# Converting weight pieces in pairs of 1024 columns, with the integer sums on GpSimd: a fused attention and feed-forward kernel on one Trainium2 core

## The chip, the cores and the metric

The kernel runs on 1 core of one Trainium2 chip. A core has TensorE (PE: matrix products; PEld is its loading of weights), VectorE (DVE), ScalarE (ACT), GpSimd (POOL) and SyncE (SP, which here issues nearly all DMAs). Each engine works through its own list of instructions in order and waits on semaphores for the others. SBUF is the on-chip memory of 128 partitions, PSUM the accumulators that TensorE writes. The metric is device time in microseconds (us); a run's time is compared as a median of several.

## The reference: what is computed

Eight batches of eight heads of linear attention without softmax, normalized per head, and then a feed-forward block with a squared relu on 4608 tokens (d_model 512, d_ff 2048):

```python
kv = np.einsum('bhsd,bhse->bhde', k, v)
out = np.einsum('bhsd,bhde->bhse', q, kv)
rms = np.sqrt(np.mean(out * out, axis=-1, keepdims=True) + 1e-06)
x = (out / rms * g_norm)            # then (B,H,S,D) -> (B*S, H*D)
h = x @ w_in
g = np.maximum(h, 0.0) ** 2
y = g @ w_out
```

q, k, v are float32 of shape (8, 8, 576, 64). The two weight matrices, 512 x 2048 and 2048 x 512, come as float64. [...] 

## The kernel before

**Stages.** The tokens are worked through in nine strips of 512. While strip 0 goes through the first product (`up_first`, L892 to L907), the weights are loaded and converted; from strip 1 on the products use Strassen-like sums of blocks of the weights, which are computed once, on the way, and stored in DRAM for streaming (`w_out`, `w_deep`). From about 132 us on, one strip follows another in the same way until the end.

**Pieces.** The weights are cut into 32 pieces of 128 partitions x 512 numbers (`sources`, L233): 16 of w_in (four column groups g, four row chunks) and 16 of w_out (two halves eh, eight j). A piece of raw 64-bit words takes 4 KB per partition; the pool `raw` has eight places, so SP loads up to eight pieces ahead (`load_piece`, L237; `load_more`, L286). The first four pieces are converted one at a time among the work of strip 0's attention (`first_piece`, L600). The other 28 are converted two at a time by `convert_pieces` (L277), 14 pairs, which I number 2 to 15 as the pieces go.

**The conversion of a piece.** ScalarE makes the absolute value of the high word, read as a float, into a tile `w_c` (L254), and the scaled low word, rounded to an integer, in place of the raw low word (L258). VectorE then does four operations (L266 to L275): clamp, shift and mask, take in the sign bits of the high word, and add the integer from the low word. The last is the integer sum; its result is the float32 number, put where it is needed. On VectorE this sum shows in the profile as an operation on 1024 halves of words (CUSTOM_DVE_ANT_0 on uint16). In `convert_pieces` the four operations of the two pieces alternate: first of one, first of the other, second of one, and so on. ScalarE is sent its work one pair ahead of VectorE.

**What the pieces are for.** Pairs 2 to 7 are w_in: pair 2 and 3 are group 1, pairs 4 and 5 group 2, pairs 6 and 7 group 3. A unit of `up_first` (16 units, each of four products with 512 columns) reads one group, the first two products the group's first pair, the other two its second. A unit's PSUM tile comes from a pool of four (`fpsum`), so a unit can't begin before the relu and the two squares of the unit four earlier (L905, L907, on ScalarE) have emptied theirs. Pairs 8 to 11 are the first half of w_out (`pieces_out`), stored into free parts of the `w_in` tile and used as weights directly. Pairs 12 to 15 are the second half (`sums_out`, L312): each piece is converted into a tile `wt`, and four differences of 128 x 256 per piece (L317 to L323; the profile shows them at L292, the helper `minus`) give the blocks that strips use; four of them go to DRAM by four DMAs a pair (L325).

**Order.** The order of instructions on every engine is written out by hand. In strip 0's loop (L1376 on) step i runs unit i, and the conversion of a pair is put behind the units 0 to 3, ahead of the units 4 to 9, and behind the units 11 and 13 to 15 (L1380, L1408, L1468). After unit 15 come the products with w_out (`down`, L997), and with them on VectorE the sums of activations (L886), norms of the next tokens, further sums of weights (`w_t`, `w_in`), and the additions of results (L1031).

Of the kernel before, what the change touches and what calls it, by code (L numbers as in the profile page):

```python
# [10 lines left out]
FP32 = mybir.dt.float32  # L11
I32 = mybir.dt.int32
U32 = mybir.dt.uint32
I64 = mybir.dt.int64
AF = mybir.ActivationFunctionType
ALU = mybir.AluOpType
# [4 lines left out]
def kernel(  # L21
# [34 lines left out]
    nc = tc.nc  # L56
    P = 128
# [4 lines left out]
    NP = H // 2  # L62
# [27 lines left out]
    c_pool = ctx.enter_context(tc.tile_pool(name="c", bufs=6))  # L90
    conv = ExitStack()
    xt_pool = conv.enter_context(tc.tile_pool(name="xt", bufs=1))
    raw_pool = conv.enter_context(tc.tile_pool(name="raw", bufs=8))
    spare_pool = conv.enter_context(tc.tile_pool(name="spare", bufs=1))
    wtmp = conv.enter_context(tc.tile_pool(name="wtmp", bufs=4))
    psums = ExitStack()
    fpsum = psums.enter_context(tc.tile_pool(name="fpsum", bufs=4, space=bass.MemoryType.PSUM))
    opening = ExitStack()
# [110 lines left out]
    def drip_queries():  # L209
# [5 lines left out]
    KH, FH, DH = NP // 2, d_ff // 2, d_model // 2  # L215
    FQ = FC // 2
    WN = 512
    NG = FQ // 2

    w_in = wpool.tile([P, KH, NG, 7, WN // 2], FP32, name="w_in")  # L220

    w_out = dram.tile([7, P, 2, FQ, P], FP32, name="w_out")
# [5 lines left out]
    w_out_11, w_out_21, w_out_t1 = w_first = [  # L228
        w_in[:, :, :, b].rearrange("p k g e -> p (k g) e") for b in (4, 5, 6)
    ]  # L230
    w_in_v = moe_w_in.rearrange("(kc p) (b g f) -> kc g p b f", p=P, b=2, g=NG)
    w_out_v = moe_w_out.rearrange("(b j p) (eh e) -> eh j p b e", p=P, b=2, eh=2)
    sources = [w_in_v[kc, g] for g in range(NG) for kc in range(NP)]  # L233
    sources += [w_out_v[eh, j] for eh in range(2) for j in range(FQ)]
    raw = []

    def load_piece():  # L237
        if len(raw) < len(sources):
            t = raw_pool.tile([P, 2, WN // 2], I64, name="raw", tag="raw")
            nc.sync.dma_start(out=t, in_=sources[len(raw)])  # L240
            raw.append(t)


    LEAST, MOST = 2.0**-15, float.fromhex("0x1.DFFFFEp+16")

    words, acted = {}, [0]

    def convert_on_act(i, parts=(0, 1)):
        view = lambda dt: raw[i].bitcast(dt).rearrange("p b (n two) -> p b n two", two=2)
        low, high, high_f = view(U32)[:, :, :, 0], view(I32)[:, :, :, 1], view(FP32)[:, :, :, 1]  # L250
        r = view(I32)[:, :, :, 0]
        if 0 in parts:
            c = wtmp.tile([P, 2, WN // 2], FP32, name="w_c", tag="w_c")
            nc.scalar.activation(c, high_f, AF.Abs)  # L254
            words[i] = c, r, high

        if 1 in parts:
            nc.scalar.activation(r, low, AF.Copy, scale=2.0**-29)  # L258

    def conversion(i, dest, eng=nc.vector):  # L260

        c, r, high = words.pop(i)
        ci = c.bitcast(I32)


        yield eng.tensor_scalar(out=c, in0=c, scalar1=LEAST, scalar2=MOST, op0=ALU.max, op1=ALU.min)  # L266

        yield nc.vector.tensor_scalar(
            out=ci, in0=ci, scalar1=3, scalar2=0x3FFFFFFF, op0=ALU.logical_shift_left, op1=ALU.bitwise_and
        )  # L270

        yield nc.vector.scalar_tensor_tensor(
            out=ci, in0=high, scalar=-(2**30), in1=ci, op0=ALU.bitwise_and, op1=ALU.bitwise_or
        )
        yield nc.vector.tensor_tensor(out=dest.bitcast(I32), in0=ci, in1=r, op=ALU.add)  # L275

    def convert_pieces(ids, dests):  # L277

        for i in range(acted[0], min(ids[-1] + 3, len(sources))):
            convert_on_act(i)  # L280
            acted[0] = i + 1
        for _ in zip(*[conversion(i, dest) for i, dest in zip(ids, dests)]):
            pass
        load_more(ids[-1] + 1)

    def load_more(end):  # L286

        while len(raw) < min(end + 8, max(len(sources) - 4, end + 4), len(sources)):
            load_piece()

    def minus(eng, out, a, b):
        eng.tensor_tensor(out=out, in0=a, in1=b, op=ALU.subtract)  # L292

    def pieces_in(i):
        g, kc = divmod(i, NP)
        b = kc // KH * 2
        convert_pieces((i, i + 1), [w_in[:, kh, g, b : b + 2] for kh in range(KH)])

    def sums_in(g):

# [5 lines left out]
        minus(nc.vector, a21, a11, a21)  # L306

    def pieces_out(j):
        dest = lambda j: w_in[:, j // NG, j % NG, 4:6]
        convert_pieces((NG * NP + j, NG * NP + j + 1), [dest(j), dest(j + 1)])  # L310

    def sums_out(j):  # L312
        js = (j, j + 1)
        t = [raw_pool.tile([P, 4, DH], FP32, name="wt", tag="raw") for _ in js]
        convert_pieces([NG * NP + FQ + j for j in js], [x[:, 0:2, :] for x in t])
        for x, j in zip(t, js):
            minus(nc.vector, w_out_t1[:, j, :], x[:, 0], w_out_11[:, j, :])  # L317
        for x, j in zip(t, js):
            minus(nc.vector, x[:, 2], x[:, 1], w_out_t1[:, j, :])
        for x in t:  # L320
            minus(nc.vector, x[:, 0], x[:, 1], x[:, 0])
        for x, j in zip(t, js):
            minus(nc.vector, x[:, 3], w_out_21[:, j, :], x[:, 2])  # L323
            for e in range(2):
                nc.sync.dma_start(out=w_out[3:7, :, e, j].rearrange("b p e -> p b e"), in_=x[:, :, ts(e, P)])  # L325

    conversions = [(pieces_in, i) for i in range(0, NG * NP, 2)]
    conversions += [(pieces_out, j) for j in range(0, FQ, 2)] + [(sums_out, j) for j in range(0, FQ, 2)]
    converted = [NP // 2]

# [25 lines left out]
    for p in range(2, NP):  # L356
        load(0, p, nc.sync, "q")
        load_piece()
        load(0, p, nc.sync, "kv")
        next(to_load)  # L360
# [239 lines left out]
    def first_piece(i, n):  # L600

        if i not in first_steps:
            first_steps[i] = conversion(
                i, w_in[:, i % KH, 0, i // KH * 2 : i // KH * 2 + 2], nc.gpsimd if i else nc.vector
            )
        for _ in range(n):
            next(first_steps[i])
# [74 lines left out]
    def sums_x(s):  # L682
# [10 lines left out]

    act, T, K, Q, N, F, piece = (
        convert_on_act, transposed_query, key_value, first_queries, first_normalized, first_features, first_piece
    )
    U = first_up
    size, low = (lambda i: (act, (i, (0,)))), (lambda i: (act, (i, (1,))))
# [7 lines left out]
    def query_pairs(b):  # L706
        first_n = b // 2 * PAIR + (C if b % 2 else 0)
        ns = list(range(first_n, first_n + C + b % 2))
        return [ns[i : i + 2] for i in range(0, len(ns), 2)]
# [9 lines left out]
    T, K, last = transposed_query, key_value, query_pairs(1)[2]  # L719
# [624 lines left out]
    attend(ready[0])  # L1344
    opening.close()
    apsum = psums.enter_context(tc.tile_pool(name="apsum", bufs=2, space=bass.MemoryType.PSUM))
    for i in range(NP, NP + 2):
        convert_on_act(i)
    acted[0] = NP + 2
    for s in range(N_STRIP):  # L1350
        attend(ready[s])
        if s == DEEP_UP - 1:
# [23 lines left out]
        for i, (w, fn, a) in enumerate(steps):  # L1376
# [33 lines left out]
            if s:  # L1410
                clock[0] += 3.2 if i >= n_up else 2.2 if s == DEEP else 1.2
                soon = tiles_due and tiles_due[0][2][0] // NT == s + 1
                if i == n_up + 10:
                    while tiles_due and tiles_due[0][2][0] // NT == s + 1:
                        _, f, a = tiles_due.popleft()
# [38 lines left out]
            n = i + 1 - (n_up - 6)  # L1454
# [44 lines left out]
```

## Time and profile before

| what | value |
|---|---|
| three runs | 871.0, 872.51, 872.37 us; median 872.37 us |
| profiled execution | span 867.8 us from the first to the last instruction (the page gives no other time for it), 4.6 us below the median of the runs |
| granted TensorE clock | 1.00 in every stage |
| HBM read and written | 197.66 MB and 36.70 MB |
| conversions in pairs | from about 31 to 95 us of the span |

How to read it: PE is TensorE's products, PEld its weight loads, POOL is GpSimd. In a timeline row the first number is the start in us from the first instruction, the second the time from start to end, then engine, line of the kernel, operation, output<-input, shapes, and xN where N instructions of one kind follow each other; what stands in brackets is idle time ahead of it and what ended it. A row of waits tells which line of which engine waited for what: total in us, times, longest. The chain of waits follows the work back from the last instruction, at each step to what released it; its rows are start, duration, what.

### The profile page before, as it was taken

What the parts mean: (1) busy time and instruction counts of PE and PEld (TensorE: products, weight loads), DVE (VectorE), ACT (ScalarE), POOL (GpSimd) and SP (SyncE); (2) the same over time, 40 slices, a digit from 0 to 9 for tenths busy, and PEclk for the clock granted to TensorE, in tenths of its full rate; (3) what the DMA queues carried; (4) which work ended last, traced back from release to release, by engine and by line L of the source; (5) the groups of instructions that cost most, each with busy time, mean ns of one, the idle gap of its engine ahead of it and who ended that gap; (6) DMA issues with size and microseconds to landing.
All of it is one profiled execution on the core that took longest, in us unless ns stands there. A gap on an engine that the chain in (4) does not pass through costs nothing.

```text
span 867.8 us, 32590 instructions
## 1 busy us (share of the span) xinstructions
PE 858.3 (99%) x14176; PEld 803.7 (93%) x14176; DVE 721.5 (83%) x1236; ACT 352.1 (41%) x805; POOL 316.2 (36%) x321
## 2 busy tenths in 40 slices
PE   8999999999999999999999999999999999999998
PEld 7445888889999999999999999999999999999998
DVE  3999998879887996789689977897889777975887
ACT  5799251320048303750356034901491148102810
POOL 1100003630459223730574045704470447145700
PEclk9999999999999999999999999999999999999999
DMA  9998997999999997989788979997668856885583
GB/s 312 301 335 251 288 376 233 296 323 361 276 261 261 346 328 235 232 311 336 213 244 272 336 244 258 294 317 260 213 221 300 305 161 220 291 286 195 177 311 124
DMA packets 169470, 236.47 MB, mean 273 GB/s; under 512 B 78704, under 2 KB 133744, under 8 KB 161008
## 3 DMA queue, kind: packets, MB, share of 16 engines
q1 hardware_dynamic: 169024, 234.33, 83.6%
q8 instruction: 111, 1.82, 0.9%
q14 instruction: 31, 0.25, 0.1%
q10 hardware_dynamic: 304, 0.07, 0.0%
HBM read 197.66 MB, written 36.70 MB: 270 GB/s over the span
## 4 chain that ended last, share of the span: by engine, by line
PE 83%; DVE 7%; ACT 5%; DMA 4%; issue 1%; SPq 0%; DVEq 0%; ACTq 0%
PE ps_A L854 35%; PE ps_B L854 31%; PE ps_C L854 5%; PE ps_A L859 4%; PE kv_ps L437 2%; PE x_ps L473 2%; PE ps_B L859 2%; DVE w_t L292 1%; ACT raw L258 1%; ACT w_c L254 1%; DMA w_blk<-w_deep 1%; DMA w_deep<-w_t 1%; DVE wt L292 1%; DMA first_qkv<-in_v_dram 1%; DMA raw<-in_moe_w_out_dram 1%
## 5 line engine op out<-in xcount | busy, mean ns | idle before, releaser
L854 PE MATMUL ps_B<-w_blk,g_s 128*64 128x128 f32 x2016 | 122.0, 273 | 0.0
L854 PEld LDWEIGHTS ps_B<-w_blk,g_s 128*64 128x64 f32 x2016 | 112.6, 137 | 0.1
L854 PE MATMUL ps_A<-x_l,w_in 128*64 128x128 f32 x1568 | 102.4, 273 | 0.6 <-ACT snap L1317 0.6
L292 POOL TENSOR_TENSOR x_l<-xT 128x256 f32<-128x256 f32 x21 | 16.0, 764 | 230.9 <-PE ps_A L854 230.9
L854 PE MATMUL ps_B<-w_blk,gt 128*64 128x128 f32 x1504 | 94.1, 273 | 0.9 <-DMA w_blk<-w_deep 0.9
L854 PE MATMUL ps_A<-w_blk,g_s 128*64 128x128 f32 x1536 | 92.2, 273 | 0.0
L854 PEld LDWEIGHTS ps_A<-x_l,w_in 128*64 128x64 f32 x1568 | 88.9, 137 | 0.9 <-ACT snap L1317 0.8
L1312 POOL TENSOR_TENSOR snap<-snap,gt 128x512 f32<-128x512 f32 x35 | 46.3, 1322 | 112.3 <-ACT snap L1317 102.7
L854 PEld LDWEIGHTS ps_B<-w_blk,gt 128*64 128x64 f32 x1504 | 84.6, 137 | 1.4 <-PE ps_B L854 1.1
L854 PEld LDWEIGHTS ps_A<-w_blk,g_s 128*64 128x64 f32 x1536 | 85.7, 137 | 0.0
L1317 ACT COPY snap<-ps_A 128x512 f32<-128x512 f32 x63 | 36.9, 585 | 103.8 <-PE ps_A L854 96.6
L1252 ACT ACTIVATE gt<-gt 128x512 f32<-128x512 f32 x112 | 70.1, 626 | 9.5 <-DVE gt L1312 9.5
L1253 ACT ACTIVATE gt<-gt 128x512 f32<-128x512 f32 x112 | 70.7, 631 | 3.6
L854 PE MATMUL ps_A<-w_blk,gt 128*64 128x128 f32 x1152 | 71.2, 273 | 0.0
L1101 ACT COPY o_sb<-ps_A 128x128 f32<-128x128 f32 x24 | 6.4, 266 | 144.9 <-PE ps_A L854 115.5
L854 PEld LDWEIGHTS ps_A<-w_blk,gt 128*64 128x64 f32 x1152 | 64.7, 137 | 0.0
L1100 DVE TENSOR_TENSOR o_sb<-o_sb,ps_B 128x256 f32<-128x256 f32 (+1 forms) x123 | 47.4, 386 | 15.0 <-ACT o_sb L1101 9.8
L292 DVE TENSOR_TENSOR gt<-gt 128x2048 f32<-128x2048 f32 (+1 forms) x29 | 59.7, 2063 | 0.0
L1312 POOL TENSOR_TENSOR gt<-gt,snap 128x512 f32<-128x512 f32 x42 | 52.6, 1283 | 15.0 <-DVE snap L1312 15.0
L854 PE MATMUL ps_B<-x_l,w_blk 128*64 128x128 f32 x784 | 51.2, 273 | 0.0
L854 PE MATMUL ps_A<-x_l,w_blk 128*64 128x128 f32 x784 | 51.2, 273 | 0.0
L1101 ACT COPY o_sb<-ps_B 128x128 f32<-128x128 f32 x31 | 8.3, 266 | 96.5 <-PE ps_B L854 96.5
(196 smaller groups left out, 1836.5 us busy)
## 6 DMA issues: line engine op xcount, KB each, us to landing
w_blk<-w_deep SPq DMA_DIRECT2D x56, 1024.0 KB, 7.4
w_blk<-w_out SPq DMA_DIRECT2D x56, 768.0 KB, 6.6
w_blk<-w_in_deep SPq DMA_DIRECT2D x49, 768.0 KB, 5.9
raw<-in_moe_w_in_dram SPq DMA_DIRECT2D x16, 512.0 KB, 7.4
raw<-in_moe_w_out_dram SPq DMA_DIRECT2D x16, 512.0 KB, 4.9
k<-in_k_dram SPq DMA_DIRECT2D x29, 256.0 KB, 5.4
v<-in_v_dram SPq DMA_DIRECT2D x29, 256.0 KB, 6.0
x_d<-x_q SPq DMA_DIRECT2D x27, 256.0 KB, 5.2
```

Of the source, the lines that this page charges most:

```text
L254: nc.scalar.activation(c, high_f, AF.Abs)
L292: eng.tensor_tensor(out=out, in0=a, in1=b, op=ALU.subtract)
L437: nc.tensor.matmul(ps[ts(h, D), i], lhsT=a, rhs=w, start=i == 0 and c == 0, stop=c == C, skip_group_check=True)
L473: nc.tensor.matmul(ps[half, r, i, ts(p, D)], lhsT=q[row, half], rhs=kvd[b, p][row, row], start=True, stop=True)
L854: nc.tensor.matmul(ps[half], lhsT=lhsT[:, half], rhs=rhs, start=start, stop=stop, skip_group_check=True)
L859: nc.tensor.matmul(bank[BANK[p]][:, i, :], lhsT=lhsT(k), rhs=rhs(k), start=p in (1, 5, 2) and i == 0 and k == 0, stop=k == n - 1, skip_gro ...
L1100: add = lambda out, a, b: nc.vector.tensor_tensor(out=out, in0=a, in1=b, op=ALU.add)
L1101: yield nc.scalar.copy(q[:, 3:4], small(1))
L1252: nc.scalar.activation(o, o, AF.Relu)
L1253: nc.scalar.activation(o, o, AF.Square)
L1312: add = lambda eng, out, a, b: eng.tensor_tensor(out=out, in0=a, in1=b, op=ALU.add)
L1317: nc.scalar.copy(t, ps)
```

## The change

Two pieces share one tile of raw words ([128, 2, 2, 256] 64-bit numbers; four such tiles for eight single ones) and one `w_c` tile of 1024 columns (two for four). For the 14 pairs each ScalarE operation covers both pieces, as do VectorE's first three operations. The fourth, the integer sum, is one operation of 1024 columns on GpSimd, for all pairs but the last, whose sum is one operation of 1024 columns on VectorE. The four differences of a `sums_out` pair each cover both pieces, and are issued one pair later: those of pair 12 behind the conversion of pair 13, and so on; those of pairs 14 and 15 behind the conversion of pair 15. The first four pieces are converted one at a time as before. Loads, stores, their sizes and the loop's steps are as they were.

```diff
-    raw_pool = conv.enter_context(tc.tile_pool(name="raw", bufs=8))
+    raw_pool = conv.enter_context(tc.tile_pool(name="raw", bufs=4))
-    wtmp = conv.enter_context(tc.tile_pool(name="wtmp", bufs=4))
+    wtmp = conv.enter_context(tc.tile_pool(name="wtmp", bufs=2))
...
+            if i % 2 == 0:
+                raw_pairs.append(raw_pool.tile([P, 2, 2, WN // 2], I64, name="raw", tag="raw"))
+            t = raw_pairs[i // 2][:, i % 2]
+            nc.sync.dma_start(out=t, in_=sources[i])
...
+    def act_words(c, view, parts=(0, 1)):
+        low, high_f, r = view(U32)[..., 0], view(FP32)[..., 1], view(I32)[..., 0]
+        if 0 in parts:
+            nc.scalar.activation(c, high_f, AF.Abs)
+        if 1 in parts:
+            nc.scalar.activation(r, low, AF.Copy, scale=2.0**-29)
...
+    def convert_pair_on_act(n):
+        view = lambda dt: raw_pairs[n].bitcast(dt).rearrange("p a b (n two) -> p a (b n) two", two=2)
+        c = wtmp.tile([P, 2, WN], FP32, name="w_c", tag="w_c")
+        act_words(c, view)
+        pair_words[n] = c, view(I32)[..., 0], view(I32)[..., 1]
...
-        yield nc.vector.tensor_tensor(out=dest.bitcast(I32), in0=ci, in1=r, op=ALU.add)
+        yield add_eng.tensor_tensor(out=dest.bitcast(I32), in0=ci, in1=r, op=ALU.add)
...
-        for i in range(acted[0], min(ids[-1] + 3, len(sources))):
-            convert_on_act(i)
-            acted[0] = i + 1
-        for _ in zip(*[conversion(i, dest) for i, dest in zip(ids, dests)]):
-            pass
-        load_more(ids[-1] + 1)
+    def convert_pair(n, dest, add_eng=nc.gpsimd):
+        for i in range(acted[0], min(n + 2, len(sources) // 2)):
+            convert_pair_on_act(i)
+            acted[0] = i + 1
+        deque(conversion(pair_words.pop(n), dest, add_eng=add_eng), 0)
+        load_more(2 * n + 2)
...
     def sums_out(j):
+        x = raw_pool.tile([P, 2, 4, DH], FP32, name="wt", tag="raw")
+        last = j + 2 == FQ
+        convert_pair((NG * NP + FQ + j) // 2, side(x[:, :, 0:2, :]), nc.vector if last else nc.gpsimd)
+        left_out.append((x, slice(j, j + 2)))
+        while len(left_out) > (0 if last else 1):
+            left_sums(*left_out.pop(0))
+
+    def left_sums(x, js):
+        minus(nc.vector, w_out_t1[:, js, :], x[:, :, 0], w_out_11[:, js, :])
+        minus(nc.vector, x[:, :, 2], x[:, :, 1], w_out_t1[:, js, :])
+        minus(nc.vector, x[:, :, 0], x[:, :, 1], x[:, :, 0])
+        minus(nc.vector, x[:, :, 3], w_out_21[:, js, :], x[:, :, 2])
+        for i in range(2):
             for e in range(2):
-                nc.sync.dma_start(out=w_out[3:7, :, e, j].rearrange("b p e -> p b e"), in_=x[:, :, ts(e, P)])
+                nc.sync.dma_start(out=w_out[3:7, :, e, js.start + i].rearrange("b p e -> p b e"), in_=x[:, i, :, ts(e, P)])
...
-    for i in range(NP, NP + 2):
-        convert_on_act(i)
-    acted[0] = NP + 2
+    convert_pair_on_act(NP // 2)
+    acted[0] = NP // 2 + 1
```

## The prediction

> **What bounds the kernel now.** I read the page's busy shares first, then busy time by stage, then the waits of TensorE's weight loads, then the chain of waits, and last the rows of VectorE and GpSimd one by one.
>
> ```profile
> span 867.8 us, 32590 instructions
> PE 858.3 (99%) x14176; PEld 803.7 (93%) x14176; DVE 721.5 (83%) x1236; ACT 352.1 (41%) x805; POOL 316.2 (36%) x321
> ```
>
> TensorE is full nearly everywhere: only 867.8 - 858.3 = 9.5 us of the span are free. By stage (columns: stretch, its length, busy time of PE, PEld, DVE, ACT, POOL with counts, granted clock, DMA share, GB/s):
>
> ```profile
> 20.00:31.00 11.00, 10.40 (x34) 5.03 (x34) 10.04 (x23) 6.18 (x13) 5.86 (x3) 1.00 1.00 299
> 31.00:69.00 38.00, 37.45 (x107) 16.53 (x108) 36.96 (x79) 36.66 (x75) 0.00 (x0) 1.00 0.96 313
> 69.00:95.00 26.00, 25.87 (x205) 16.63 (x204) 26.00 (x65) 19.42 (x46) 0.80 (x1) 1.00 0.94 278
> 95.00:132.00 37.00, 36.74 (x238) 31.86 (x237) 35.90 (x64) 12.78 (x15) 0.00 (x0) 1.00 0.97 340
> ```
>
> The paired conversions run from 31 to 95 us. There VectorE is as full as TensorE, and it stays full to 132 us; GpSimd is empty. So two engines are critical side by side: VectorE time saved here can win only TensorE's gaps, VectorE time added comes out at the end. Three waits show how close they are (31 to 132 us; total, times, longest):
>
> ```profile
> PEld ps_A L900 <- DVE w_in L275: 1.6, 3, 1.0
> PEld ps_B L900 <- ACT gt L907: 1.1, 1, 1.1
> PEld ps_A L859 <- DVE o_sb L1031: 0.7, 1, 0.7
> ```
>
> The chain goes along VectorE to the third and from there along TensorE:
>
> ```profile
> 129.25 1.89 DVE w_t L292 x3
> 131.15 0.61 DVE o_sb L1031
> 131.80 8.90 PE ps_A L859 x40
> ```
>
> What one pair costs VectorE now: four operations on each of two pieces, one pair per 3.75 us (47.19 to 50.94):
>
> ```profile
> 47.19 0.76 DVE L266 TENSOR_SCALAR w_c<-w_c 128x512 f32<-128x512 f32 x2
> 47.86 0.75 DVE L268 TENSOR_SCALAR w_c<-w_c 128x512 int32<-128x512 int32 x2
> 48.53 1.28 DVE L272 SCALAR_TENSOR_TENSOR w_c<-raw,w_c 128x512 int32<-128x512 int32 x2
> 49.73 1.28 DVE L275 CUSTOM_DVE_ANT_0 w_in<-raw,w_c 128x1024 uint16<-128x1024 uint16 x2
> 50.94 0.75 DVE L266 TENSOR_SCALAR w_c<-w_c 128x512 f32<-128x512 f32 x2
> ```
>
> The decisive rows are later, where GpSimd adds float tiles beside VectorE:
>
> ```profile
> 142.95 1.28 POOL L1208 TENSOR_TENSOR w_i<-w_in 128x512 f32<-128x512 f32 x1 [58.93 <-DMA out_dram<-o_sb]
> 143.36 1.42 DVE L923 SCALAR_TENSOR_TENSOR gt<-gt 128x512 f32<-128x512 f32 x1
> 146.47 1.33 DVE L292 TENSOR_TENSOR w_t<-w_blk 128x512 f32<-128x512 f32 x1
> 147.21 1.72 POOL L1208 TENSOR_TENSOR w_i<-w_in 128x512 f32<-128x512 f32 x1
> 168.23 0.91 DVE L540 TENSOR_SCALAR ms<-ms 128x16 f32<-128x16 f32 x1
> ```
>
> L923 takes 0.69 us where GpSimd is idle. Here GpSimd's sum ends at 144.23 and L923 at 144.78: it stood still until GpSimd was done and needed 0.55 us more. GpSimd's sum of 147.21 stood in turn until VectorE's of 146.47 ended (147.80) and needed 1.13 us more of its usual 1.28. L540, a tensor_scalar with its operands in SBUF, takes 0.17 us alone and 0.91 here, ending with the GpSimd sum of 167.85 (1.26 us). Operations that read PSUM, reductions and transposes keep their time. So a GpSimd tensor_tensor and VectorE's SBUF tensor_tensor, scalar_tensor_tensor and tensor_scalar run one after the other, and these are all that a conversion consists of.
>
> **The change, part by part.** *Three VectorE operations of 1024 columns for six of 512.* A 512 tensor_tensor takes 0.684 us and a 2048 one 2.283 (L292, gt), 0.53 us per 512 more, so the scalar_tensor_tensor takes 0.68 + 0.53 = 1.22; the tensor_scalars (0.42 at 512) take 0.70, with 0.28 per 512 after the 0.14 that overlaps a neighbour. Each now waits for the one before, where two pieces alternated: as in the single piece (22.65 + 0.42, next at 23.10) that is 0.03 more. Alone: 0.70 + 0.70 + 1.22 = 2.6 us a pair.
>
> *The integer sum leaves VectorE.* It frees 2 x 0.6 = 1.2 us a pair, 13 of 14 pairs.
>
> *It goes to GpSimd.* No integer sum of GpSimd is in the trace. Nearest is its float tensor_tensor: 0.73 us at 256 columns and 1.28 at 512, so 1.28 + 2 x 0.55 = 2.4 at 1024, of which 2.4 - 0.14 = 2.24 shuts VectorE out. The slow bound is its tensor_scalar (L266, 1.92 at 512): 3.8. The low bound is that nothing or little of the sum shuts VectorE out: while L266 ran on GpSimd from 24.8 to 26.7, VectorE's L268 at 25.52 took its normal 0.42 and L272 at 25.97 its 0.69. I take 2.4 with full exclusion, since operation and count of inputs are the same and those rows hold without an exception.
>
> The Trainium skill, SBUF — State Buffer, section "SBUF: two separate sides", says that whichever of the two engines starts first has the shared ports for its whole instruction and the other blocks fully. The float sums agree (0.55 us after GpSimd's end); the one-input L266 does not, it let VectorE pass before its end. By the page the sum below stands; if the integer sum behaved as L266 does, the second rival would.
>
> *Period.* VectorE's 0.56 + 0.56 + 0.17 + 1.08 (0.17: one wait between dependents that nothing fills) and GpSimd's 2.24 make 4.6 us a pair, 4.9 if all three VectorE operations go ahead of the sum; before, 3.75.
>
> *Sums of the last four pairs.* Before 8 x 0.335 = 2.7 us a pair, now 4 x 0.65 = 2.6, shifted by a pair so that they don't wait for GpSimd; they need SBUF alone and are shut out too. The last integer sum stays on VectorE: 1.2.
>
> *VectorE to the end of the sums.* Before 31.3 to 95.4: 64.1 us. Now 14 x 2.37 = 33.2, plus 1.2, plus 4 x 2.6 = 10.4, plus 13 x 2.24 = 29.1 of exclusion: 73.9, and about 1 for the later start (the 1024 Abs must end first: 31.8 for 31.3) and handovers: 75. That is 11 us later.
>
> *ScalarE* issues two 1024 activations for four of 512: 0.684 at 512 and 2.0 at 2048 (L301) give 1.12 each, 0.2 to 0.3 us a pair less. But with two double buffers the Abs of pair n+2 waits for GpSimd's sum of pair n, and behind it stand the relu and squares (1.26 us) that free PSUM for the unit four later. ScalarE then goes at 4.6 us a unit where TensorE needs 3.43 (41.05 to 44.48). Pair 2's Abs ends at 31.8, its VectorE part at 34.5, its sum at 36.9; pair 3's VectorE part, shut out until then, ends at 39.5, one tensor_scalar of pair 4 slips in, and its sum ends at 42.2. TensorE began the half that reads it at 39.22: 3 us lost. Pair 10's sum comes at 42.2 + 7 x 4.6 = 74.4, Abs and Copy behind it take 2.1, relu and squares 1.3: 77.8 for the unit that began at 71.26, 6.5 lost. This lies inside the 11.
>
> *SP's queue.* The same 32 loads and 16 stores. A load of a pair waits for both pieces' sum, so SP stands 2 to 3 us longer at first, and behind it are the key, value and query loads, used 30 us later. Loads keep four pairs, 18 us, ahead against 7 us of flight. Nothing.
>
> *Path to the end.* After the sums VectorE is 97% busy to 132 (35.90 of 37.00), so its delay reaches L1031 undiminished, and TensorE, which already waits there, is 11 us late. Earlier the products from w_blk (109.61) need the stores behind the last sum (last landing 101.6, reload issued 101.61): 11 less about 1 of slack. Same delay, not added. After 132 TensorE is full (731.5 of 736) and gives nothing back.
>
> Sum: 867.8 + 11 = 879 us of span. The page gives no other time of its execution; the median of the three runs, 872.37, is 4.6 above it. So **883 us**. With 3 us less (hidden in the 132 us) to 4 more (period 4.9) and a little besides, its own range is 877 to 889.
>
> **The rivals.** *Slow integer sum.* At 3.8 us 13 sums shut VectorE out for 1.46 more: 11 + 19 = 30 us, 902. For it: L266's row. Against it: one addition, not two operations.
>
> *Little exclusion.* The integer sum lets go early as L266 does, 0.6 us. VectorE then needs 33.2 + 1.2 + 10.4 + 7.8 = 53 us for what ScalarE and TensorE pace to 60 anyway. Pair 3 still comes by Abs 35.1, three operations 37.7, sum 40.1, against 39.22: 0.9 lost. The ScalarE wait (0.46 us of TensorE's start, 54.77 due, 55.23 seen) and L1031's go: about 0.9 won. 872.4, within 0.2%.
>
> *Faster.* No exclusion, and pair 3's sum comes by 39.2 (a GpSimd sum of 1.5 us or less decides). What can be won is TensorE's free time from 31 to 132, 0.94 us by the table, and starts shown late by 0.1 between units, some 2.4 in all: 870. For it: the work does leave the full engine. Against it: every row of two-input sums.
>
> **How the numbers follow.** A measurement of this kernel can tell about 0.2%, 1.7 us. Forecast 0.70, slow sum 0.10, little exclusion 0.13, faster 0.07. Slower is 0.80, same 0.13, faster 0.07. From 872 to 893 leaves out the faster case, half of the little-exclusion case and most of the slow one: 0.20.
>
> **What would show it.** GpSimd sums of 2.4 us or more one per 4.6 us from 34 to 90; VectorE's tensor_scalars mixed, 0.7 free and near 2.8 beside a sum; TensorE waiting for the integer sum at 42 and for L907 afterwards; the conversion's last sum at 106 instead of 95, L1031 at 142. Wrong would be: VectorE operations of 0.70 and 1.22 while GpSimd sums run (second rival or faster); sums of 3 us and more without waiting (the first).

## The result

The changed kernel takes 884.2 us (median of 4 runs, 881.36 to 888.56) beside 871.68 us for the kernel before (4 runs, 870.28 to 872.51): a ratio of 1.0157, 95% interval 1.0125 to 1.0189. It is slower by 12.5 us; 883 was forecast. The profiled execution took 884.8 us with a span of 883.0, so 1.8 us lie around the span.

The busy times on the profile's page of the changed kernel:

```profile
span 883.0 us, 32459 instructions
PE 860.9 (97%) x14176; PEld 804.2 (91%) x14176; DVE 727.3 (82%) x1151; ACT 350.2 (40%) x777; POOL 350.2 (40%) x334
```

VectorE has 85 instructions fewer and is busy 5.8 us longer (721.5 before); GpSimd gained 34 us. TensorE's idle time rose from 9.5 to 883.0 - 860.9 = 22.1 us. The next view tells where. Busy time by stage, columns as in the prediction (PE, PEld, DVE, ACT, POOL with counts, granted clock, DMA share, GB/s):

```profile
31.00:69.00 38.00, 31.71 (x75) 13.15 (x75) 36.33 (x26) 28.21 (x42) 20.33 (x8) 1.00 0.87 273
69.00:95.00 26.00, 23.13 (x118) 11.85 (x119) 24.30 (x21) 19.38 (x37) 11.53 (x5) 1.00 0.55 180
95.00:106.00 11.00, 11.00 (x131) 9.48 (x130) 8.57 (x13) 6.00 (x13) 3.17 (x2) 1.00 1.12 329
106.00:146.00 40.00, 36.41 (x233) 30.85 (x232) 37.56 (x66) 12.88 (x15) 0.00 (x0) 1.00 0.97 331
```

Look at DVE from 31 to 69: 26 instructions fill 36.33 us, where 79 filled 36.96. One third of the instructions takes the same time, so each is either doing twice the work or standing still. TensorE's free time in the four stages (length less PE) is 6.3, 2.9, 0 and 3.6 us: it is lost where the conversions run, and once more ahead of 146. Rows of VectorE, GpSimd and TensorE from the timeline (start, time from start to end, engine, line, operation, output<-input, shapes, count; in brackets the idle time ahead and what ended it) tell what VectorE does. L279 and L281 are the two tensor_scalars, L285 the scalar_tensor_tensor, L288 the integer sum:

```profile
34.34 2.40 POOL L288 TENSOR_TENSOR w_in<-w_c,raw 128x1024 int32<-128x1024 int32 x1 [7.91 <-ACT gt L925]
34.77 2.52 DVE L279 TENSOR_SCALAR w_c<-w_c 128x1024 f32<-128x1024 f32 x1 [0.57 <-ACT w_c L255]
...
39.41 2.70 POOL L288 TENSOR_TENSOR w_in<-w_c,raw 128x1024 int32<-128x1024 int32 x1 [2.67 <-DVE w_c L285]
...
42.17 1.99 PE L918 MATMUL ps_A<-xT,w_in 128*128 128x512 f32 x4 [3.39 <-POOL w_in L288]
...
42.70 1.22 DVE L285 SCALAR_TENSOR_TENSOR w_c<-raw,w_c 128x1024 int32<-128x1024 int32 x1
43.84 0.69 DVE L279 TENSOR_SCALAR w_c<-w_c 128x1024 f32<-128x1024 f32 x1
44.05 2.72 POOL L288 TENSOR_TENSOR w_in<-w_c,raw 128x1024 int32<-128x1024 int32 x1 [1.94 <-DVE w_c L285]
44.56 2.76 DVE L281 TENSOR_SCALAR w_c<-w_c 128x1024 int32<-128x1024 int32 x1
47.36 1.23 DVE L285 SCALAR_TENSOR_TENSOR w_c<-raw,w_c 128x1024 int32<-128x1024 int32 x1
```

Pair 2's sum starts at 34.34 with VectorE idle and takes 2.40 us. The clamp that VectorE starts at 34.77 takes 0.69 us when nothing stands in its way (43.84), and ends here at 37.29, 0.55 us behind the sum's end at 36.74. From then on, up to pair 11, every period looks like 42.70 to 47.36: one clamp slips through, one sum of 2.72 (it waits for the clamp), and the shift of 44.56 stands 2.76 us for 0.69 of work, ending 0.55 after the sum. The period is 4.66 us. At 42.17 TensorE gets the half that pair 3's sum writes, after a gap of 3.39 us.

What TensorE's weight loads wait for from 30 to 150 us (total, times, longest), without the rows of "issue", which name no releaser:

```profile
PEld ps_A L918 <- POOL w_in L288: 5.3, 4, 4.2
PEld t_ps L424 <- ACT qT L429: 3.4, 1, 3.4
PEld ps_A L918 <- ACT gt L925: 1.8, 1, 1.8
PEld ps_A L877 <- DVE gt L304: 1.7, 1, 1.7
PEld ps_B L918 <- ACT gt L925: 1.7, 1, 1.7
PEld ps_A L877 <- DVE o_sb L1049: 1.5, 1, 1.5
```

The integer sum is at the top. In TensorE's timeline the gaps of the four stages are 3.39 us for pair 3's sum, 3.20 in five waits for squares (L925), 2.57 ahead of 79.84, where transposes wait for ScalarE's copy (`qT`, L429), and 3.35 in three waits for VectorE behind the conversions: 12.5 of the 12.8 us. The chain of waits passes through the late end of the sums, `g_s` at 107.25 for 95.51, and reaches TensorE through the same `o_sb` addition, 13.05 us later than before (144.20 for 131.15). (A timeline starts each of these `g_s` rows 0.09 us earlier, at 107.16 and 95.42; the experiments below give starts of the timeline.)

```profile
107.25 2.41 DVE g_s L904 x4
...
144.20 0.61 DVE o_sb L1049
144.86 5.23 PE ps_A L877 x23
```

The delay grows on the way, from 11.74 us at `g_s` to 13.05 at `o_sb`. VectorE stands for a store there, which it did not before:

```profile
129.00 0.69 DVE L304 TENSOR_TENSOR w_t<-w_in 128x512 f32<-128x512 f32 x1 [1.33 <-DMA w_deep<-w_t]
```

### The profile page after: what moved, and what is told of

It reads as the page before. It is cut to its first block, busy times and chain, and to the rows that moved or that the text cites. A ratio compares the mean times of both kernels' runs of the same rounds, so it can differ in the third digit from the quotient of the medians.

```text
span 883.0 us, 32459 instructions
## 1 busy us (share of the span) xinstructions
PE 860.9 (97%) x14176; PEld 804.2 (91%) x14176; DVE 727.3 (82%) x1151; ACT 350.2 (40%) x777; POOL 350.2 (40%) x334
## 4 chain that ended last, share of the span: by engine, by line
PE 80%; DVE 9%; DMA 5%; ACT 3%; issue 1%; POOL 1%; SPq 1%; DVEq 0%; POOLq 0%
PE ps_A L872 34%; PE ps_B L872 30%; PE ps_C L872 4%; PE ps_A L877 4%; DVE w_c L281 2%; PE x_ps L491 2%; PE kv_ps L455 2%; PE ps_B L877 2%; DVE w_t L304 1%; DVE w_c L285 1%; DMA w_deep<-w_t 1%; DMA w_blk<-w_deep 1%; DVE wt L304 1%; DVE w_c L279 1%; DMA first_qkv<-in_v_dram 1%
```

## The experiments

A ratio below is to runs of the kernel before that belong to the same experiment (their medians were 870.24, 871.0 and 870.85 us); it is given as recorded, with its 95% interval, and is not the quotient of the two medians. Diffs are against the changed kernel unless said otherwise. The theory throughout: GpSimd's integer sum shuts VectorE out while it runs. The rivals put the loss on the widening to 1024 columns, on the two `w_c` buffers, on GpSimd's speed, or on the transfers.

**Wide operations, all on VectorE.**

```
-    def convert_pair(n, dest, add_eng=nc.gpsimd):
+    def convert_pair(n, dest, add_eng=nc.vector):
...
-        convert_pair(..., side(x[:, :, 0:2, :]), nc.vector if last else nc.gpsimd)
+        convert_pair(..., side(x[:, :, 0:2, :]), nc.vector)
```

> The changed kernel with all integer sums back on VectorE, 1024 columns wide; ScalarE's and VectorE's wide operations, the tiles and the shifted differences stay. Exclusion theory (a GpSimd sum with two SBUF inputs and VectorE's conversion operations run one after the other, 4.65 us a pair): without GpSimd a pair costs VectorE 0.70 + 0.70 + 1.22 + 1.22 and three waits of 0.03, 3.9 us against 3.75 before, so 14 x 0.15 = 2 us over the kernel before, 872 to 876. Rival, widening (three dependent wide operations, with nothing to alternate with, and the wide double buffers cost the time): most of the 13 us stay, 880 or more.

Measured: 895.77 us, 1.0261 (1.0206 to 1.0316), slower even than the change. A row of its timeline tells why the number can't be read as the widening's price:

```profile
48.27 1.22 DVE L288 CUSTOM_DVE_ANT_0 w_in<-raw,w_c 128x2048 uint16<-128x2048 uint16 x1 [3.08 <-PE ps_C L918]
```

The conversion's sum waits 3.08 us for TensorE, and in the waits TensorE's products wait for it in turn, 9.1 us at the longest. The weights that those products read are not the ones this sum writes; the destination is two stretches of `w_in`, one per half, and the order seems to be kept against what lies between them too. It came in with the edit (GpSimd's sum into the same place shows no such wait), so the sum was split, and with that these waits are gone.

**Wide operations, the sum on VectorE piece by piece.** As above, and

```
+        if len(dest.shape) == 3 and dest.shape[-1] == WN:
+            for i in range(2):
+                nc.vector.tensor_tensor(out=dest[:, i].bitcast(I32), in0=ci[:, i], in1=r[:, i], op=ALU.add)
+            return
         yield add_eng.tensor_tensor(out=dest.bitcast(I32), in0=ci, in1=r, op=ALU.add)
```

> As wide_dve, but VectorE's integer sum of a w_in pair goes piece by piece (two of 512 columns), so that what it writes is one stretch of the tile. In wide_dve the profile shows VectorE's wide sum of one column group waiting for TensorE's products of another, and TensorE for that sum, which no exact account of the data asks for; the wide sum's destination spans both row halves with other groups between them. Theory: that false order cost wide_dve its time, and widening itself costs the 0.15 us a pair of wide_dve's expectation: 871 to 876. Rival, widening: stays at 880 or more.

Measured: 876.4 us, 1.0058 (1.0035 to 1.0081; 10 runs). Between both expectations. One pair on its VectorE:

```profile
47.25 0.69 DVE L279 TENSOR_SCALAR w_c<-w_c 128x1024 f32<-128x1024 f32 x1
47.97 0.69 DVE L281 TENSOR_SCALAR w_c<-w_c 128x1024 int32<-128x1024 int32 x1
48.70 1.23 DVE L285 SCALAR_TENSOR_TENSOR w_c<-raw,w_c 128x1024 int32<-128x1024 int32 x1
50.06 1.29 DVE L290 CUSTOM_DVE_ANT_0 w_in<-raw,w_c 128x1024 uint16<-128x1024 uint16 x2
51.27 0.69 DVE L279 TENSOR_SCALAR w_c<-w_c 128x1024 f32<-128x1024 f32 x1
```

The period is 4.02 us, where two interleaved pieces took 3.75. From start to start the steps are 0.72, 0.73, 1.36, 1.21, against 0.67, 0.67, 1.20, 1.21 before. A wide operation is hardly shorter than two narrow ones behind each other (0.69 for 0.76, 1.23 for 1.28), and each now waits for the one ahead of it, while two pieces in turn filled each other's wait. So the widening saves VectorE nothing, it costs 0.27 us a pair. `g_s` starts at 100.75, 5.3 us late; on the way there pair 14's sum waits 3.28 us for a store, to which I come back.

**The sums on GpSimd, without the widening.** Against the kernel before:

```
-        yield nc.vector.tensor_tensor(out=dest.bitcast(I32), in0=ci, in1=r, op=ALU.add)
+        yield add_eng.tensor_tensor(out=dest.bitcast(I32), in0=ci, in1=r, op=ALU.add)
...
+        add_eng = nc.gpsimd if ids[0] < NG * NP + FQ else nc.vector
+        for _ in zip(*[conversion(i, dest, add_eng=add_eng) for i, dest in zip(ids, dests)]):
```

> The kernel before with one part of the change alone: the integer sums of the pairs 2 to 11 go to GpSimd, 512 columns each; all the rest stays as before, the last four pairs' sums on VectorE. Exclusion theory: a pair takes VectorE's 2 x (0.335 + 0.335 + 0.60) = 2.5 us and two shares of 1.14 that a float sum of 512 shuts out, 4.8 us against 3.75, ten pairs: about 10 us more than before, 879 to 885. Rival, widening: nothing wide is here and 1.2 us a pair left VectorE, so no slower than before, 869 to 873.

Measured: 879.77 us, 1.0092 (1.006 to 1.0124), as the theory said: 0.9% lost with ten of the pairs moved and every buffer as before. Its timeline:

```profile
42.36 3.06 POOL L275 TENSOR_TENSOR w_in<-w_c,raw 128x512 int32<-128x512 int32 x2 [1.69 <-DVE w_c L272]
42.75 2.95 DVE L266 TENSOR_SCALAR w_c<-w_c 128x512 f32<-128x512 f32 x2
45.62 0.75 DVE L268 TENSOR_SCALAR w_c<-w_c 128x512 int32<-128x512 int32 x2
```

The two clamps, 0.76 us together before, take 2.95 beside two sums of GpSimd. The period is 4.75 us. Moving the sum alone makes the pair longer than the change does (4.75 us for 4.66), and `g_s` starts at 103.84, 8.4 us late: the move is enough for a loss, without the widening.

**GpSimd's operation with one input.** The integer sum is replaced by a clamp of `w_c` into the same place; the low word's part and the sum are left out.

```
+        if add_eng is nc.gpsimd:
+            yield nc.gpsimd.tensor_scalar(out=dest, in0=c, scalar1=LEAST, scalar2=MOST, op0=ALU.max, op1=ALU.min)
+            return
```

> The changed kernel with each GpSimd sum replaced by a GpSimd tensor_scalar (clamp) of 1024 columns that reads the same w_c tile alone and writes the same place: longer work on GpSimd (3.8 us by L266's 1.92 at 512) but one input. It leaves out the low word's part of the numbers. Exclusion theory, with the row of before in which L266 let VectorE pass: VectorE's operations keep 0.70 and 1.22, GpSimd's own 3.9 us a pair set the pace instead of 4.65; pair 3 comes at about 42 as with the sum (3 us lost), then little is added: 874 to 878. Rival, length (a GpSimd stage in the chain costs by its length, whatever its inputs): 13 x 1.4 us more than the change, 900 or more.

Measured: 873.17 us, 1.0031 (1.0016 to 1.0047; 10 runs), a little under what the theory gave. This is the sharpest of the runs, since GpSimd works longer here than in the change:

```profile
41.57 7.28 POOL L289 TENSOR_SCALAR w_in<-w_c 128x1024 f32<-128x1024 f32 x2 [0.32 <-DVE w_c L285]
42.47 0.69 DVE L279 TENSOR_SCALAR w_c<-w_c 128x1024 f32<-128x1024 f32 x1 [0.97 <-ACT w_c L255]
43.19 0.69 DVE L281 TENSOR_SCALAR w_c<-w_c 128x1024 int32<-128x1024 int32 x1
43.92 1.23 DVE L285 SCALAR_TENSOR_TENSOR w_c<-raw,w_c 128x1024 int32<-128x1024 int32 x1
```

Each GpSimd operation takes 3.6 us, and VectorE's three beside it keep their lone times; `g_s` starts at 97.98. These three start 0.9 us or more into GpSimd's operation, since VectorE waits for ScalarE ahead of each pair. In the last pairs VectorE has work throughout, and there two operations a pair do stand:

```profile
78.56 3.94 POOL L289 TENSOR_SCALAR wt<-w_c 128x1024 f32<-128x1024 f32 x1 [2.90 <-ACT qT L432]
79.05 1.40 DVE L307 TENSOR_TENSOR wt<-wt,w_in 128x512 f32<-128x512 f32 x1
81.58 1.46 DVE L279 TENSOR_SCALAR w_c<-w_c 128x1024 f32<-128x1024 f32 x1
```

Both take 0.69 us alone, and the clamp ends at 83.04, 0.54 us behind GpSimd's end at 82.50. The two together lose 1.5 us; what lies between them (80.38, 80.98) keeps its 0.68. So the one-input operation can shut VectorE out too, but only for a part of its time.

With the same shapes, buffers and order and a slower GpSimd, most of the loss is gone (873.17 for 884.2). So the loss is neither GpSimd's pace nor the hand-over between engines: it is that the sum keeps VectorE standing for nearly all its length. This run's operation differs from the sum in its inputs (one for two), its instruction and its number type. The float sums of the kernel before shut VectorE out as well, so the number type alone is not it; no run separates the other two.

**The sum issued twice.**

```
+        if add_eng is nc.gpsimd:
+            yield add_eng.tensor_tensor(out=dest.bitcast(I32), in0=ci, in1=r, op=ALU.add)
         yield add_eng.tensor_tensor(out=dest.bitcast(I32), in0=ci, in1=r, op=ALU.add)
```

> The changed kernel with each GpSimd sum issued twice (same operands, same result). GpSimd is idle 1.95 us of every 4.65 in the change. Exclusion theory: this idle time is VectorE's turn, nothing of a second sum can hide in it, so every pair takes 2.2 to 2.4 us more, 13 pairs: 29 us over the change, 909 to 917. Rival, length or widening: the second sum fits mostly into GpSimd's idle time, 884 to 892.

Measured: 910.94 us, 1.046 (1.0429 to 1.0491), as the theory said. 13 more sums cost 910.94 - 884.2 = 26.7 us, 2.06 each; shut-out of 2.24 each would have been 29. In its timeline VectorE's clamp of 47.49 takes 2.93 us beside the first sum, and beside the second the shift takes 2.76:

```profile
49.95 2.71 POOL L290 TENSOR_TENSOR w_in<-w_c,raw 128x1024 int32<-128x1024 int32 x1
50.46 2.76 DVE L281 TENSOR_SCALAR w_c<-w_c 128x1024 int32<-128x1024 int32 x1
```

**Four `w_c` tiles.**

```
-    wtmp = conv.enter_context(tc.tile_pool(name="wtmp", bufs=2))
+    wtmp = conv.enter_context(tc.tile_pool(name="wtmp", bufs=4))
```

> The changed kernel with four instead of two w_c tiles, so that ScalarE's Abs of a pair no longer waits for the GpSimd sum two pairs ahead, and the relu and squares behind it come early. Exclusion theory, with the prediction's claim that ScalarE's path lies inside VectorE's delay: TensorE's waits for L925 between 54 and 77 us go (about 5 us of it), but the last sum of the conversions still ends near 107 and L1049 near 144, and the time stays within 3 us of the change: 881 to 886. Rival, buffers (the two tiles and ScalarE's wait are what costs): 872 to 876.

Measured: 883.58 us, 1.0132 (1.0094 to 1.0171). TensorE's waits for squares between 54 and 73 us (0.3 to 0.9 each in the change, 3.2 together) are gone, and others of 2.11 and 2.27 us come later (96.2 and 111.4); `g_s` starts at 106.93 for 107.16. So ScalarE's path is real and lies inside VectorE's delay, and the two buffers aren't the cause.

**Where pair 14's sum waits.** In the change GpSimd stands 8.6 us for a store, and behind it VectorE 2.29. Two rows of its timeline:

```profile
97.80 3.12 POOL L288 TENSOR_TENSOR wt<-w_c,raw 128x1024 int32<-128x1024 int32 x1 [8.60 <-DMA w_out<-wt]
...
100.96 1.23 DVE L288 CUSTOM_DVE_ANT_0 wt<-raw,w_c 128x2048 uint16<-128x2048 uint16 x1 [2.29 <-POOL xT L1459]
```

`wt` tiles live in the pool of the raw tiles, of which there are four where there were eight halves, and the differences and stores of a pair now come a pair later. A new `wt` waits until stores have left. Two edits take it apart: leave the last pairs' sums on VectorE, or give the pool a fifth tile.

```
-        convert_pair(..., side(x[:, :, 0:2, :]), nc.vector if last else nc.gpsimd)
+        convert_pair(..., side(x[:, :, 0:2, :]), nc.vector)
```

> The changed kernel with the integer sums of the pairs 12 to 14 on VectorE as well (as pair 15's is); pairs 2 to 11 stay on GpSimd. Exclusion theory: three sums that shut VectorE out for 2.24 become three of 1.2 on VectorE, 3 us earlier at the end of the conversions; up to pair 11 nothing changes: 879 to 883. Rival (the time is lost in the last four pairs, by the shift of the differences and the waits for tiles there): back to 875 or less.

Measured: 883.86 us, 1.0134 (1.0094 to 1.0174). The exclusion is gone from the last four pairs, and `g_s` starts at 107.26 all the same: the store wait, now VectorE's own, holds what was won.

```profile
94.57 1.23 DVE L288 CUSTOM_DVE_ANT_0 wt<-raw,w_c 128x2048 uint16<-128x2048 uint16 x1 [3.26 <-DMA w_out<-wt]
```

```
-    raw_pool = conv.enter_context(tc.tile_pool(name="raw", bufs=4))
+    raw_pool = conv.enter_context(tc.tile_pool(name="raw", bufs=5))
```

> The changed kernel with five instead of four raw tiles. In the change GpSimd's sum of pair 14 waits 8.6 us, at last for a store of the shifted differences, VectorE's sum of pair 15 stands 2.3 us behind it, and the Abs of pair 15 waits 3.9 us for its load. Theory: this is a second loss, in the last four pairs, of 2 to 4 us, beside the exclusion: 880 to 883. Rival: the waits are covered, since VectorE has differences to do: no change, 883 to 886.

Measured: 883.14 us, 1.0132 (1.0086 to 1.0179). The store wait is gone, and in the timeline an exclusion stands in its place, a difference of 0.69 us that takes 2.77 beside pair 14's sum:

```profile
93.60 2.62 POOL L288 TENSOR_TENSOR wt<-w_c,raw 128x1024 int32<-128x1024 int32 x1 [4.57 <-ACT ps_C L923]
94.01 2.77 DVE L304 TENSOR_TENSOR wt<-wt,w_in 128x512 f32<-128x512 f32 x1
```

`g_s` starts at 106.94. Neither edit alone moves the end. Both together:

> The edits of raw_five and pool_w_only together: five raw tiles, and VectorE does the integer sums of the pairs 12 to 15, GpSimd those of 2 to 11. Each alone left the end of the conversions at 107: with five tiles the wait for the store went and VectorE stood 2.1 us shut out by pair 14's sum instead; with VectorE's sums the exclusion went and the wait for the store was 3.3 us. Theory: either covers the other, so only both together win, 3.3 us at the end of the conversions (104): 879 to 881.5. Rival: something else sets the last four pairs' pace (loads or ScalarE): again 883 to 886.

Measured: 880.12 us, 1.0107 (1.0072 to 1.0142; 5 runs). Now the chain moves:

```profile
104.32 2.49 DVE L904 TENSOR_TENSOR g_s<-gt 128x512 f32<-128x512 f32 x4
```

2.8 us earlier than in the change (107.16). The median is 4.1 us lower, but the intervals of the two ratios overlap, so it is the chain that shows the gain and not the time. Store wait and exclusion were each other's cover. What stays, 104.32 - 95.42 = 8.9 us, is as much as pairs 2 to 11 lose by their period, 10 x (4.66 - 3.75) = 9.1.

**Only ScalarE wide.** VectorE converts the two halves in turn as before, sums included, and the differences aren't put off:

```
-        deque(conversion(pair_words.pop(n), dest, add_eng=add_eng), 0)
+        of, help_eng = pair_words.pop(n), nc.vector
+        halves_of = [[t[:, i] for t in of] for i in range(2)]
+        for _ in zip(conversion(halves_of[0], dest[:, 0]), conversion(halves_of[1], dest[:, 1], help_eng)):
+            pass
...
-        while len(left_out) > (0 if last else 1):
+        while left_out:
```

> The changed kernel's tiles, loads and wide ScalarE operations, its differences over both pieces, but VectorE's four operations piece by piece, alternating, the integer sum among them on VectorE, and the differences not shifted. So it is the kernel before with ScalarE alone in pairs. Theory (what hurts is GpSimd's sum, and a little the lost alternation and the shift): VectorE needs 3.75 us a pair as before, ScalarE 0.25 us a pair less, so TensorE's wait for L907 (0.46) goes: 869 to 871.5, with 871 before. Rival (the tiles in pairs cost by themselves, through later loads and freed places): 873 or more.

Measured: 872.11 us, 1.0011 (0.9991 to 1.0031; 12 runs): no difference that can be told. `g_s` starts at 94.77, 0.65 us earlier than before, but TensorE now waits 1.69 us for squares at 52.61. They stand on ScalarE behind a wide pair of activations whose load was late (3.44 us idle ahead of the first, at 49.16). And VectorE stands 1.04 us for a store of `w_t` at 116.31, so that `o_sb` starts 0.36 us later than before (131.42 for 131.06). So the wide activations alone win nothing that can be told.

**And half of the clamps on GpSimd.** As the last, with `help_eng = nc.gpsimd if 4 <= n < (NG * NP + FQ) // 2 else nc.vector`: the second half's clamp, an operation with one input, in eight pairs.

> As act_pairs, with the clamp of the second piece of the pairs 4 to 11 on GpSimd (a tensor_scalar of 512 columns, one input, 1.9 us), so that VectorE has 0.34 us a pair less and GpSimd's work shuts it out little. Theory: VectorE ends the conversions up to 2.5 us earlier, TensorE wins what it still waits for, 0.5 us: 868.5 to 871. Rival (any GpSimd work beside VectorE shuts it out for its length): 1.9 us a pair more on VectorE, 877 or more.

Measured: 874.88 us, 1.0037 (1.0019 to 1.0054; 12 runs). A miss: I had expected a gain.

```profile
53.50 2.46 POOL L279 TENSOR_SCALAR w_c<-w_c 128x512 f32<-128x512 f32 x1 [1.60 <-ACT w_c L255]
```

```profile
54.10 1.70 DVE L288 CUSTOM_DVE_ANT_0 w_in<-raw,w_c 128x1024 uint16<-128x1024 uint16 x2
55.72 0.51 DVE L279 TENSOR_SCALAR w_c<-w_c 128x512 f32<-128x512 f32 x1
```

The first fence is GpSimd's timeline, the second VectorE's. The pair of sums at 54.10 takes 1.70 us, 1.29 elsewhere, and the clamp 0.51 for 0.42. Such a clamp shuts VectorE out for some 0.4 to 0.5 us. Moving it off VectorE saves less: from clamp to shift it is 0.45 us (43.76 to 44.21) where two clamps take 0.67. So the period is 3.95 us (43.76 to 47.71) for 3.75, where I had counted on 0.34 less, and `g_s` starts at 96.83, 2.1 us later than with the clamps on VectorE.

No version beat the kernel before.

## Why the prediction was right

*Exclusion* held as worked out: 0.55 us of VectorE's operation after each sum's end, forecast from the float sums' rows, and seen here for integers. The Trainium skill, SBUF — State Buffer, section "SBUF: two separate sides", has the shared ports locked for a whole instruction, the other engine fully blocked. The two-input sums agree (2.76 us for 0.69 of work), and the one-input operations do not (0.69 us kept beside GpSimd's 3.6 in most pairs, 0.7 to 0.8 us lost by each of two operations in the last pairs).

*The sum's 2.4 us* was exact: 2.40 where it doesn't wait, 2.70 where it has VectorE's operation ahead. The slow-sum rival fell with it. *The period* was 4.66 for 4.6. *VectorE's operations*, 0.70, 0.70 and 1.22, measured 0.69, 0.69 and 1.23. What I did not see is in the run with the sums split: the wait between dependents that I took as 0.03 is 0.13 ahead of the integer sum (49.93 to 50.06; it is 0.03 to 0.04 ahead of the others), so without GpSimd the wide form would be the slower one by 0.27 us a pair. In the change this is covered, since VectorE stands for GpSimd anyway.

*Pair 3's sum* was to end at 42.2 and cost TensorE 3 us: it ended at 42.11, TensorE's gap was 3.39. *ScalarE's path lies inside the 11*: right by the run with four `w_c` tiles, but its size was too small. The unit that began at 71.26 begins at 80.34, 9.1 us late where 6.5 was worked out; the difference is the transposes' wait for ScalarE's copy (2.57 us), which I had not followed.

*The end of the sums* was forecast at 106 and came at 107.25, 11.7 us late for 11. *SP's queue, "Nothing"* is a step that failed. I priced the loads and looked at no wait of a `wt` tile for stores, though the change halves the number of tiles and puts the stores off by a pair. It was there, 8.6 us of GpSimd's time and 2.29 of VectorE's. Yet taking it away alone moved `g_s` by 0.2 us, since an exclusion that I had in the sum took its place. So the item was missed and the total hardly suffered. The loads were not on time either: the Abs of pair 15 waits 3.94 us for its load (94.67), but VectorE's clamp behind it (95.99) follows the differences without a gap, so this cost nothing here.

*After 132 nothing is given back, and nothing more is lost* failed by some 3 us. TensorE starts behind `o_sb` 13.06 us later than before (144.86 for 131.80), 1.3 more than `g_s`: that is VectorE's wait for the store of `w_t`, 1.33 us, another store that I had not priced. From there to the end the idle time is 6.14 us for 4.30, most of the difference at 263 us (1.16 us, absent before) and at 302 (1.11 for 0.87). No run tests what moved these.

*The time around the span* was wrong as well, and it hid these: I added 4.6 us, the distance from the profiled span to the median before. The changed kernel's own profiled execution has 1.8 there, and so has every other run here (1.8 to 2.2, the later runs of the kernel before included). So the span was forecast 4.2 us too short (878.8 for 883.0) and the time around it 2.8 too long. That 883 came within 1.2 us of 884.2 is in part luck; the mechanism and its 11 us are not. With 1.9 us around it, an estimate from those runs, the profiled execution before took some 869.7 us, 2 less than the median of 871.68, and part of the 15.2 us by which the span grew is that; by the medians the change cost 12.5 us where 883 - 872.37 = 10.6 was forecast.

*Little exclusion and faster* were refuted for this sum by the same rows. The rival with little exclusion forecast 872.4, and the one-input run, which has little, gave 873.17: the case was priced about rightly, and of these two GpSimd operations it is the one with two inputs that holds VectorE nearly throughout.

## What to carry to other kernels

Before work is moved from a full VectorE to an idle GpSimd, look in the trace for a two-input operation of GpSimd beside VectorE work in SBUF: if VectorE's operations beside it always end shortly after it (0.55 us here), the engines take turns, and the move adds nearly GpSimd's whole time (2.2 of 2.4 us) to take away VectorE's (1.2). Two half-width chains in turn can be faster than one of full width, because each fills the other's wait for its own result (3.75 against 4.02 us a pair). When a removed wait moves nothing, look for what stood behind it and take both away.

## What was not expected of the hardware

TensorE's granted clock fell at the gap of 38 to 42 us in some executions and not in others. Busy time by stretches of 4 us, first the change, then the run with five raw tiles; the columns are as above, the clock the third from the end:

```profile
38.00:42.00 4.00, 0.78 (x2) 0.00 (x0) 3.93 (x4) 2.18 (x5) 2.59 (x1) 1.00 0.89 263
42.00:46.00 4.00, 3.83 (x9) 1.82 (x10) 3.93 (x4) 3.37 (x5) 2.06 (x2) 1.00 0.98 296
```

```profile
38.00:42.00 4.00, 0.61 (x3) 0.03 (x1) 3.96 (x3) 2.06 (x5) 2.70 (x1) 0.83 1.03 342
42.00:46.00 4.00, 4.00 (x5) 1.82 (x6) 3.93 (x4) 3.30 (x5) 2.14 (x1) 0.50 1.09 345
```

The gap was 3.39 us in both, and only the second lost half its clock (5 products started from 42 to 46 us for 9). Read in steps of 0.1 us, the clock there falls to 0.50 at 40.65, 2.1 us after TensorE went idle, and is back at 47.45, 6.8 us later. In the run with the sums issued twice it falls at 40.2, when products have run again for 1.3 us behind a gap of 2.59, and is back at 50.4, 10.2 us later. With four `w_c` tiles it falls at 43.3, 1.0 us behind the gap, for 3.4 us.

The Trainium skill, TensorE: Matmul & The Clock Gate, section "Part 1: The HAM clock gate (the "warmup" mystery)", has the clock halved after an idle window of about 3.4 us in a window that runs freely. The lengths agree: they are once, twice and three times 3.4 us. That one gap of 3.39 us halves the clock and another doesn't agrees too. That the window has to be idle throughout doesn't: the clock fell after 2.1 us of idleness, and behind a gap of 2.59. Where the limit lies isn't shown; a gap of 2.63 us left the clock at 1.00 in the run with 512-column sums on GpSimd.

The clock doesn't explain the spread of the changed kernel's runs: their spans of 883.0, 879.5, 881.8 and 886.7 us don't follow their mean clocks (1.0, 0.996, 0.996, 0.996), and what makes the spread stays open.

That a one-input operation of GpSimd shuts VectorE out for a part of its time was new to me, but a row of the kernel before has it. Beside GpSimd's clamp of 19.99 to 21.91 VectorE's L491 takes 0.63 us, and 0.17 at 25.44:

```profile
20.00 0.63 DVE L491 TENSOR_SCALAR ms<-ms 128x8 f32<-128x8 f32 x1
```

In the run with half of the clamps on GpSimd it was 0.4 to 0.5 us at 512 columns, in the run with one input 1.5 at 1024.
